# Sixty-four narrow dummy matmuls in place of thirty-two wide ones at the opening of an attention and MLP kernel

## The chip, the cores and the metric

The kernel runs on one core of one Trainium2 chip. The metric is the device time of one execution in microseconds (us); lower is better. Three runs of the kernel before took 103.33, 104.07 and 104.88 us, the median being 104.07. A further execution was taken with the hardware profiler; every row below is from that one.

## The reference

Attention with quadratic sketched features, for 4 batches of 4 heads, 1088 tokens and 32 columns a head, followed by a two-layer network on the 4352 tokens. Cut to what matters:

```python
def phi(x):                                    # S1, S2: 8 x 32
    a = einsum('rd,bhsd->bhsr', S1, x)
    b = einsum('rd,bhsd->bhsr', S2, x)
    return einsum('bhsi,bhsj->bhsij', a, b).reshape(..., 64)
q_p, k_p = phi(q), phi(k)
kv  = einsum('bhsf,bhsd->bhfd', k_p, v)
z   = sum(k_p, axis=2)
num = einsum('bhsf,bhfd->bhsd', q_p, kv)
den = einsum('bhsf,bhf->bhs', q_p, z)[..., None] + 1e-06
x   = (num / den) as 4352 x 128                # heads side by side
h   = x @ w_in                                 # 128 x 2048
out = (h - tanh(h)) @ w_out                    # 2048 x 128
```

Inputs and outputs are float32.

## The kernel before

**How it is staged.** Batch 0 is prepared first, in the opening, in two chunks of queries (16 blocks of 32 tokens, then 18). The network then runs over groups of up to 512 tokens (`layers`), and the attention of batches 1, 2 and 3 is made between the network's matmuls. In the opening, TensorE ("PE") turns the sketches into weights (`sketch`, L605), projects the keys (L704, two parts, "keys0" and "keys1"), spreads S2 (L628), makes the Gram matrix (L729), projects the first queries (L883), folds (L781), and sums key features times values (L748, "sums0" and "sums4"). ScalarE ("ACT") copies that sum (`kvz`, L807), PE transposes the copy (L816), ACT copies it back (`ndw`, L824), and PE multiplies the query features by it (L1007, "nd0" and "nd1", after VectorE's ("DVE") transposes `qpT`, L944). Their result `xT` is cast by ACT and DVE (L1022), and the network's first layer can start: L1114 multiplies by `w_in` into PSUM, ACT takes the tanh (L1124), and L1143 (or L1139 for the last, smaller groups) multiplies by `w_out`. The linear part, h itself times w_out, is folded into one 128 by 128 matrix: `w_in` is transposed in two halves of eight matmuls (L1048), DVE copies each half (L1055), and sixteen matmuls (L1062) make the product, which L1083 applies.

**Dummy matmuls.** `warm` (L597) issues matmuls on a zero tile `wz` whose result nobody reads. `FILLS = 29, 3, 0, 1, 0, 0, 4, 4` says how many stand in each of eight places: 29 before `sketch` ("fill0"), 3 after it ("fill1"), one before the Gram matrix, 4 before the transposes L816 ("fill6") and 4 after them ("fill7"). All are 128 by 128 on 128 columns.

**Who sets the order.** A planner in the kernel's own code (`Program.schedule`, `listed`) builds one list for each engine. For the opening, `LINE` writes each engine's order out by hand, dummies included; from there on the planner chooses by due times and its own cost figures. Its figures also treat TensorE's program as coming in pieces: `PACKET = 256` records a piece, counted from 63 (`count, packets = 63, [0, 0]`), each operation having `ni` records. One matmul of the source is two records, a weight load and a matmul, and for float32 operands four. When the count enters a piece, the planner books the arrival of the piece after the next one, 5,300 ns later in the first 16,500 ns and 3,300 ns later afterwards:

```python
                if count // PACKET != (count + o.ni) // PACKET:
                    packets.append(o.at + (SLOW if o.at < BUSY else FETCH))
                count += o.ni
```

**Queues.** Nearly all loads and stores are issued by SyncE ("SP") in one order. After the loads of batch 0 come w_in (L538) and w_out (L543), then k, q and v of batch 1, which wait for `ndw` of batch 0 (L824). GpSimd ("POOL") casts the second half of w_in (L550) and both halves of w_out (L554); ACT casts the first half of w_in after `ndw`.

Of the kernel before, what the change touches and what calls it, by code (L numbers as in the profile page):

```python
# [51 lines left out]
W_GATE = "wu", 0  # L52
GATE1 = "ndw", 0
WK_POOL = 0
FILLN = 128
FILLS = 29, 3, 0, 1, 0, 0, 4, 4
GPS = ("wk", 1, 0, 0), ("wk", 1, 1, 0), ("qp", 0, 1), ("w_in", 2), ("w_in", 3), ("w_out", 0)
LINE = {
# [343 lines left out]
def bass_polysketch_attn__then__act_tanh_shrink_kernel(nc, q, k, v, S1, S2, moe_w_in, moe_w_out, out):  # L402
    P = Program(nc)

    def sb(name, shape, dtype=F32):
        return nc.alloc_sbuf_tensor(name, shape, dtype).ap()
# [16 lines left out]
    wz = sb("wz", [128, 512], BF16)  # L423
# [47 lines left out]
    ps = nc.alloc_psum_tensor("ps", [128, 8 * 512], F32).ap().rearrange("p (b n) -> p b n", b=8)  # L471
# [125 lines left out]
    def warm():  # L597
        for x, n in enumerate(FILLS):
            for _ in range(n):
                w = 128 if x else FILLN  # L600
                P.op("tensor", 54 * w // 128, lambda e, w=w: e.matmul(  # L601
                    ps[:, 6, 0:w], wz[:, 0:128], wz[:, 0:w], start=True, stop=True), r=[("wz",)], name=f"fill{x}")

    def sketch():
        P.op("tensor", 250, lambda e: e.matmul(  # L605
# [589 lines left out]
    P.bias = BIAS  # L1195
    mark = len(P.ops)
    warm()
    sketch()

# [22 lines left out]
    if LEAD:  # L1222
        for e, names in LINE.items():
            found = [[o for o in P.ops[mark:] if o.eng == e and o.name == n] for n in names]
            line = [o for f in found for o in f]
            assert all(len(f) == (FILLS[int(n[4:])] if n[0][0] == "f" and n[0:4] == "fill" else 1) for n, f in zip(names, found)), names
            for x, y in zip(line, line[1:]):
# [87 lines left out]
```

## Time and profile before

| | |
|---|---|
| three runs, median | 103.33 to 104.88 us, 104.07 us |
| the profiled execution's own time | 104.34 us |
| its span, first to last instruction | 102.2 us (so 2.1 us lie around it) |
| mean granted TensorE clock | 0.983 |
| ACT tanh, L1124 | 138 instructions, 68.9 us busy |
| L1114, 128x512 | 100 matmuls, 35.9 us busy, mean 385 ns |
| L1143, 128x512 | 110 matmuls, 35.4 us busy, mean 379 ns |
| dummy matmuls, L601 | 41 in the trace, 4.7 us busy |
| idle of PE just before L601, "issue" | 1.9 us, once |

"Busy" counts overlapping instructions of an engine once; PE's matmul ends are modelled, so what counts for PE is when one starts after another. "Granted clock" is the share of full speed that the throttle let TensorE run at. An idle time of an engine is put down to what released it; "issue" means that nothing the profile shows released it. Loads of the engines' programs show as DMA queues of the kind "instruction".

### The profile page before, as it was taken

Reading aid. Unit: us, or ns where it says so; the run is one execution under the profiler, and the core shown is the slowest. Engines: PE = TensorE matmul, PEld = TensorE weight load, DVE = VectorE, ACT = ScalarE, POOL = GpSimd, SP = SyncE. Lnnn points to the kernel's source line nnn. Section 1 sums busy time; section 2 is a strip of 40 time slices with the busy share of each in tenths; the row PEclk is TensorE's granted clock in tenths of the full one; section 3 lists DMA queues with packets and bytes.
Section 4 is the critical chain, followed back from the end, with each engine's and each line's share of the span. In section 5 each row is a group of like instructions: output and inputs, shape, how many; then the busy total and the mean of one; then the engine's idle time right before and its main releaser. Section 6 shows DMA issues by size and latency. Waiting matters only on the chain.

```text
span 102.2 us, 3488 instructions
## 1 busy us (share of the span) xinstructions
PE 93.8 (92%) x1505; PEld 56.2 (55%) x1519; DVE 60.7 (59%) x122; ACT 75.1 (74%) x154; POOL 34.5 (34%) x39
## 2 busy tenths in 40 slices
PE   5999389999999999999999999999999999999980
PEld 5888265564365543344447554344343454699980
DVE  3688935499838999973999941591937220042040
ACT  3131613897467892699994969999986999999960
POOL 5646445250195700099989000008800000000000
PEclk9999985999999999999999999999999999999999
DMA  2999899930018799995006150060024006003322
GB/s 49 356 199 291 240 317 375 239 81 10 0 17 244 142 255 201 203 187 76 0 0 227 18 86 3 1 102 0 0 42 65 2 6 96 0 16 61 68 51 77
DMA packets 22911, 11.24 MB, mean 110 GB/s; under 512 B 15728, under 2 KB 21104, under 8 KB 22896
## 3 DMA queue, kind: packets, MB, share of 16 engines
q1 hardware_dynamic: 22464, 10.40, 43.6%
q10 hardware_dynamic: 432, 0.62, 2.0%
q8 instruction: 12, 0.20, 0.8%
q14 instruction: 3, 0.02, 0.1%
HBM read 8.79 MB, written 2.23 MB: 108 GB/s over the span
## 4 chain that ended last, share of the span: by engine, by line
PE 69%; ACT 13%; DVE 10%; issue 4%
PE ps L1114 21%; PE ps L1143 15%; ACT tt L1124 13%; PE ps L1139 5%; PE ps L1007 5%; PE ps L601 4%; PE ps L748 3%; DVE kT L643 2%; DVE qpT L944 2%; PE ps L883 2%; PE ps L1083 2%; PE ps L1048 2%; PE ps L684 2%; PE ps L729 1%; PE ps L704 1%
## 5 line engine op out<-in xcount | busy, mean ns | idle before, releaser
L1124 ACT ACTIVATE tt<-ps 128x512 bf16<-128x512 f32 (+1 forms) x138 | 68.9, 665 | 11.2 <-PE ps L1114 5.2
L1114 PE MATMUL ps<-xT,w_in 128*128 128x512 bf16 x100 | 35.9, 385 | 2.0 <-issue 1.5
L1143 PE MATMUL ps<-tt,w_out 128*128 128x512 bf16 x110 | 35.4, 379 | 0.2 <-issue 0.2
L662 POOL TENSOR_TENSOR wk<-kab 128x1152 f32<-128x1152 f32 (+2 forms) x8 | 15.5, 1933 | 15.4 <-DVE kab L691 13.0
L1114 PEld LDWEIGHTS ps<-xT,w_in 128*128 128x128 bf16 x112 | 9.9, 98 | 15.2 <-ACT tt L1124 7.3
L1143 PEld LDWEIGHTS ps<-tt,w_out 128*128 128x128 bf16 x112 | 10.8, 98 | 11.0 <-issue 0.9
L1166 DVE STREAM_TRANSPOSE osb<-ps 128x512 f32<-128x512 f32 x7 | 5.0, 713 | 12.4 <-PE ps L1143 12.3
L1114 PE MATMUL ps<-xp,w_in 128*128 128x256 bf16 (+1 forms) x64 | 9.5, 246 | 0.1
L983 POOL TENSOR_TENSOR qp<-an,w_out_f 128x1152 f32<-128x1152 f32 x2 | 4.3, 2174 | 13.0 <-DVE an L978 12.9
L1139 PE MATMUL ps<-w_out,tt 128*128 128x128 bf16 x96 | 8.2, 219 | 0.0
L601 PE MATMUL ps<-wz 128*128 128x128 bf16 x41 | 4.7, 285 | 3.1 <-issue 1.9
L989 DVE STREAM_TRANSPOSE qpT<-qp 128x1152 f32<-128x1152 f32 x4 | 5.5, 1368 | 2.5 <-POOL qp L983 2.5
L1007 PE MATMUL ps<-qpT,ndw 32*32 32x288 f32 (+3 forms) x320 | 6.9, 352 | 0.0
L1028 DVE CAST xT<-ps 128x512 bf16<-128x512 f32 x7 | 4.5, 681 | 3.5 <-PE ps L1007 3.5
L1139 PEld LDWEIGHTS ps<-w_out,tt 128*128 128x128 bf16 x96 | 6.4, 98 | 0.1
L933 POOL TENSOR_TENSOR qp<-an,ab 128x512 f32<-128x512 f32 (+2 forms) x3 | 4.5, 1514 | 4.9 <-DVE an L928 4.9
L643 DVE STREAM_TRANSPOSE kT<-kraw 128x256 f32<-128x256 f32 (+3 forms) x10 | 5.6, 602 | 0.7 <-DMA kraw<-in_k_dram 0.7
L1114 PEld LDWEIGHTS ps<-xp,w_in 128*128 128x128 bf16 x64 | 5.0, 98 | 1.5
L851 DVE STREAM_TRANSPOSE qT<-qraw 128x512 f32<-128x512 f32 (+3 forms) x9 | 5.8, 653 | 0.0
L601 PEld LDWEIGHTS ps<-wz 128*128 128x128 bf16 x41 | 3.9, 133 | 3.5 <-issue 2.0
L944 DVE STREAM_TRANSPOSE qpT<-qp 128x512 f32<-128x512 f32 (+2 forms) x6 | 5.6, 954 | 0.1
L1007 PEld LDWEIGHTS ps<-qpT,ndw 32*32 32x32 f32 x320 | 4.0, 103 | 2.7 <-issue 1.2
(101 smaller groups left out, 96.3 us busy)
## 6 DMA issues: line engine op xcount, KB each, us to landing
kraw<-in_k_dram SPq DMA_DIRECT2D x3, 544.0 KB, 4.0
qraw<-in_q_dram SPq DMA_DIRECT2D x3, 544.0 KB, 8.0
w_in_f<-in_moe_w_in_dram SPq DMA_DIRECT2D x4, 256.0 KB, 5.6
w_out_f<-in_moe_w_out_dram SPq DMA_DIRECT2D x2, 512.0 KB, 8.0
out_dram<-osb SPq DMA_DIRECT2D x16, 64.0 KB, 2.5
vx<-in_v_dram SPq DMA_DIRECT2D x6, 144.0 KB, 6.5
vx<-in_v_dram SPq DMA_DIRECT2D x6, 128.0 KB, 7.8
vx<-in_v_dram SPq DMA_DIRECT2D x6, 64.0 KB, 3.0
```

The costliest lines, as they stand in the source:

```text
L601: P.op("tensor", 54 * w // 128, lambda e, w=w: e.matmul(ps[:, 6, 0:w], wz[:, 0:128], wz[:, 0:w], start=True, stop=True), r=[("wz",)], name ...
L643: P.op("vector", dve(hi - lo), lambda e, cb=cb, t0=t0, n=n, lo=lo, hi=hi: e.transpose(out=kT[i][:, t0:t0 + n, cb:cb + 2, :], in_=kraw[i][: ...
L662: return lambda e: e.tensor_tensor(out=wk[:, r, y0:y1, :, :].rearrange("p t h (i j) -> p (t h) i j", i=R), in0=pa[:, :, :, None].to_broadc ...
L851: P.op("vector", dve(hi - lo), lambda e, lo=lo, hi=hi: e.transpose(out=qT[i][:, lo:hi], in_=qraw[i][:, lo:hi]), r=cols("qraw", i, lo, hi), ...
L944: c.t_op = P.op("vector", dve(64 * n), lambda e, r=r: e.transpose(out=qpT[u][:, r, 0:64 * n], in_=qp[u][:, r, 0:64 * n]), r=[("qp", u, r)] ...
L989: c.t_op = P.op("vector", dve(1152), lambda e, r=r: e.transpose(out=qpT[u][:, r, :], in_=qp[u][:, r, :]), r=[("qp", u, r)], w=[("qpT", u, r)])
L1007: ins = e.matmul(ps[32 * h:32 * h + 32, k0 + s, 0:32 * own[s]], ndw[b % 2][32 * s:32 * s + 32, y, 32 * h:32 * h + 32], src, start=(y == 0) ...
L1114: o = P.op("tensor", pe(n), lambda e, jb=jb, bk=bk, y=y: e.matmul(bk[:, n * y:n * y + n], w_in[:, 128 * jb:128 * jb + 128], xs[:, 0:n], st ...
L1124: P.op("scalar", act(m), lambda e, ts=ts, bk=bk, m=m: e.activation(out=tt[:, ts, 0:m], in_=bk[:, 0:m], func=AF.Tanh, scale=-1.0), r=[kb], ...
L1139: P.op("tensor", pe(128), lambda e, jb=jb, ts=ts, o_=o_, at=n * y + at: e.matmul(o_, tt[:, ts, at:at + 128], w_out[:, jb, :], start=False, ...
L1143: P.op("tensor", pe(n), lambda e, jb=jb, ts=ts: e.matmul(acc[:, 0:n], w_out[:, jb, :], tt[:, ts, 0:n], start=(jb == 0 and not g), stop=(jb ...
L1166: P.op("vector", dve(n), lambda e: e.transpose(out=osb[u][:, 0:n], in_=acc[:, 0:n]), r=[ka], w=[("osb", u)], want=due(NJB) + LAG)
```

## The change

The dummies of the first two places become twice as many and smaller: 58 before `sketch` and 6 after it, each with 32 stationary columns (so it writes 32 partitions) and 64 moving columns. The dummies of the other places stay 128 by 128. All 128 rows of the tile still take part.

```diff
-FILLN = 128
-FILLS = 29, 3, 0, 1, 0, 0, 4, 4
+FILLN = 64
+FILLS = 58, 6, 0, 1, 0, 0, 4, 4
...
-                w = 128 if x else FILLN
-                P.op("tensor", 54 * w // 128, lambda e, w=w: e.matmul(
-                    ps[:, 6, 0:w], wz[:, 0:128], wz[:, 0:w], start=True, stop=True), r=[("wz",)], name=f"fill{x}")
+                w = 128 if x > 1 else FILLN
+                m = 128 if w == 128 else 32
+                P.op("tensor", 54 * w // 128, lambda e, w=w, m=m: e.matmul(
+                    ps[0:m, 6, 0:w], wz[:, 0:m], wz[:, 0:w], start=True, stop=True), r=[("wz",)], name=f"fill{x}")
```

The program has 64 records more before the keys, so each later piece of 256 begins 64 records sooner in the work. The planner sees that and lists some instructions elsewhere. In TensorE's list: the second eight transposes of w_in (L1048) go from before the first L1114 to after seven of them (and four L1143); DVE's second copy L1055 follows them, behind the second chunk's `qp` (L938). Before the second chunk's L1007 there are one L1114 and two L1143 more. Of batch 1, the Gram matrix (L729) comes after both L1083 and three L1114 instead of between the two L1083, and DVE's transpose of the first output group (L1166) comes before the Gram matrix's mask (L763) instead of after it. In SP's list the four stores of that output group (L1174) go ahead of the load of k for batch 2 (L517). A few other L1114 and L1143 change places up to the second batch's L1007; from there on, and on POOL throughout, the lists are the same.

## The prediction

> **What bounds the kernel now.** I read the page first, then the chain of waits, then busy time and clock by stretches, then PE's timeline around the longest "issue" wait. From the page:
>
> ```profile
> span 102.2 us, 3488 instructions
> PE 93.8 (92%) x1505; PEld 56.2 (55%) x1519; DVE 60.7 (59%) x122; ACT 75.1 (74%) x154; POOL 34.5 (34%) x39
> ...
> PEclk9999985999999999999999999999999999999999
> ...
> q8 instruction: 12, 0.20, 0.8%
> ...
> PE 69%; ACT 13%; DVE 10%; issue 4%
> ```
>
> PE carries 69% of the chain and is busy for 92% of the span, so a microsecond that it gains before 20 us mostly reaches the end. One slice has half the clock. Twelve program loads went by queue 8, 0.20 MB / 12 = 16 KB each. PE's timeline, with start, duration and the wait in brackets:
>
> ```profile
> 10.24 0.40 PE L601 MATMUL ps<-wz 128*128 128x128 bf16 x4
> 10.80 0.44 PE L816 MATMUL ps<-ident,kvz 128*128 128x128 f32 x2 [0.16 <-ACT kvz L807]
> 11.07 0.28 PE L601 MATMUL ps<-wz 128*128 128x128 bf16 x2
> 13.23 0.27 PE L601 MATMUL ps<-wz 128*128 128x128 bf16 x2 [1.89 <-issue]
> 13.44 1.15 PE L1007 MATMUL ps<-qpT,ndw 32*32 32x128 f32 x64
> ```
>
> Dummies depend on nothing but a zero tile, yet the third of four waited 1.89 us. It is PE's 444th weight load or matmul; with the four waits that stand as records of their own, 447 lie before it, and by the planner's count of 63 ahead and 256 a piece the boundary lies at 449. So I read the wait as PE's program arriving late. The trace's records of queue 8 fit: the first load's packet starts at 10.98 and takes 0.92, and PE goes on 1.33 after its end. The next is at 16.34 for 1.16. Twelve loads agree with some 3,050 PE records / 256 = 11.9 boundaries, one load for each boundary reached, so two pieces were aboard at the start and entering the second asks for the third.
>
> The clock, in stretches cut where the trace's clock records change (columns: stretch and length, busy and count of PE, weight loads, DVE, ACT, POOL, granted clock, DMA share, GB/s):
>
> ```profile
> 4.25:7.67 3.42, 3.33 (x73) 2.55 (x72) 2.90 (x10) 0.80 (x2) 1.52 (x4) 1.00 1.02 226
> 7.67:11.08 3.41, 3.25 (x127) 2.76 (x126) 2.91 (x9) 0.74 (x2) 2.13 (x4) 1.00 0.91 287
> 11.08:14.49 3.41, 1.52 (x70) 1.12 (x67) 1.79 (x4) 1.41 (x3) 1.31 (x3) 1.00 0.94 274
> 14.49:17.91 3.42, 3.20 (x28) 2.28 (x25) 2.16 (x4) 1.41 (x4) 1.84 (x3) 0.50 1.07 354
> ```
>
> The stretch with the wait has PE busy for 1.52 of 3.41, and the clock is halved through exactly the next 3.42; stretches with 3.25 and more keep it. The wait thus costs twice: 1.89 idle, and half of 3.20 = 1.6 of PE's work at half speed.
>
> **The change part by part.** Sums are against the profiled execution, 104.34 (span 102.2 and 2.1 around it), 0.27 above the median of 104.07.
>
> The new dummies. In the trace the old ones start every 107 ns until 4.2 (3.1 in all) and every 55 from 4.7 on: the clock is low up to 4.25. No row has a 32-column matmul alone. Halving the columns gives an estimated 53 ns, 58 x 53 = 3.1, as before. Bounds: 17 ns a pair (L748: 72 in 1.21, on four column groups at a time), so 1.0; and 107, so 6.2. Early gains nothing: keys1 waits for DVE's key transposes, which end at 5.70. Late has 0.2 of slack between keys0 and keys1, then goes on the path, up to +2.9. I take 0, since halving one row is nearer than either end.
>
> The program's pieces. Entering the second piece comes 64 records sooner, at what is now the 63rd pair, in L704 at 6.10, instead of the 95th, L883 at 7.49. PE's sequencer runs ahead: a wait record behind pair 29 ran while pair 13 did, so the request may come some 16 pairs sooner, at pair 47 (5.42); today it cannot come before the wait record at 7.07. From request to resumption it took 13.23 - 7.49 = 5.7 to 13.23 - 7.07 = 6.2. The third piece would thus be there at 11.1 to 12.3; I take 11.7. Further bound: later loads start about 0.3 after their boundary (21.94 to 22.21), which gives 6.1 + 0.3 + 0.9 + 1.3 = 8.6; with DMA 86 to 117% busy here I stay near the loaded row.
>
> The new boundary lies in sums4 (L748), at what is now pair 190, 9.74. The wait becomes 11.7 - 9.7 = 2.0. Today pair 190 to the end of L748 takes 0.57, and from there to the earliest L1007 through kvz, L816 and ndw 1.45 (10.30 to 11.75). So L1007 starts at 13.7 instead of 13.44: **+0.25**. The query side is ready at 12.5 (qpT 11.21 + 1.30) and hides nothing. The loads of batch 1 wait for `ndw`, now 2 us later than 11.64; SP's issue already took 2.30 instead of 0.4 there, so the queue was full, and k lands at 20.97 against its use at 23.42. I count 0; without that cover up to +0.5.
>
> The moved transposes. Eight L1048 fewer stand before the first L1114: at half clock 16 took 1.89, so -0.94; the 0.22 wait ahead of L1114 for the casts of `xT` goes as well, since ACT and DVE finish within the other eight. They return later at full clock, as 16 L1062 do (1.0 for 16): +0.5. Net **-0.66**. The DVE copy that goes with them now follows `qp`, which ends 0.6 sooner with L883 (21.52 - 0.6 = 20.9, by the 18.1 below against 18.72), so it is done at 20.9 + 0.69 = 21.6; by the new list PE needs it near 21.9 (18.1 + 3.8 of rows until L1062): hidden, by 0.3.
>
> The next boundary falls at the end of the second chunk's L883. PE is there at 13.7 + 1.1 + 0.95 + 1.3 (three L1114 at half clock) + 1.0 = 18.1; the fourth piece, asked for at 11.7 and 13.23 to 16.34 + 1.16 + 1.33 = 5.6 on the way, is there at 17.3. At full clock PE would be there near 17.0 and wait 0.3. I book **+0.1**.
>
> The replanned middle. DVE's transpose of the first output (0.71) before the mask lies beside three L1114 (0.65) and L729 (0.3): 0, without them +0.4. Four stores (2.55 of SP issue) ahead of the load of k for batch 2, today issued at 29.54, put its landing near 32.1 + 4.0 = 36.1 against its use at 35.05, with other DVE work able to follow only in order: 0 to +1.0, I take 0 as the first store may start 0.7 sooner and ACT's 2.46 idle at 26.6 shrinks. Sum: +0.25 - 0.66 + 0.1 = -0.3, with the half-clock stretch kept.
>
> One rule speaks against the mechanism itself. The Trainium skill, "Runtime: NRT & Kernel Launch", section "Instruction fetch mechanics", says that the program is refilled in blocks of 256 instructions and that crossing a block is mostly hidden. The 1.89 row disagrees; by the rule the wait had another cause, which is rival four.
>
> **Rivals.** First, the clock does not fall: the wait is cut by the 3.41 grid. On today's grid its idle lies partly before 11.08 (1.3) and partly behind (0.6 and two gaps of 0.3 around L816), so each stretch is about 2.1 busy, between 1.52, which lost the clock, and 3.25, which kept it. That saves 1.6 more: 104.0 - 1.6 = 102.4, or 101.5 if the piece also comes a microsecond sooner, when qpT bounds L1007 at 12.5. Against it, the grid need not lie so in other runs. The Trainium skill, "TensorE: Matmul & The Clock Gate", section "Why this matters for your kernels", allows idle gaps up to about 3 us, by which neither wait would cost the clock and 102.4 would be the rule; the 0.50 row, behind a gap of 1.89, disagrees.
>
> Second, slower: the fourth piece becomes the bound. It is now asked for at 11.7, with w_out (second half lands at 17.50) and then k of batch 1 (20.97) ahead of it in the DMA engines. If its packet starts only at 17.5, it is usable at 17.5 + 1.2 + 1.3 = 20.0, PE waits 1.9 from 18.1, and a second halved stretch costs up to 1.6: 104.0 + 1.9 + 0.8 = 106.7 with half of that stretch. It decides from a packet later than 15.6. For it: a full queue; against: today's packet took 3.1 in the same load.
>
> Third, narrow dummies do not release the clock at 4.25. A quarter of the array's columns works, and no row shows that alone. One stretch more at half clock costs at most 3.33 / 2 = 1.67, less 0.25 of slack: 105.4; two, 3.25 / 2 more: 107.0.
>
> Fourth, the boundary is not where I put it, the wait stays at its dummy: 104.34 - 0.66 = 103.7.
>
> **How the numbers follow.** Forecast 0.50; first rival 0.21; second 0.14; third 0.10; fourth 0.05. The forecast is 104.34 - 0.3 = 104.0, its own range 103.0 to 105.0 by the bounds of the piece's arrival (0.6 either way) and the middle. 2% of 104.07, about what a measurement of this kernel with runs 1.5% apart tells from no change, is 2.1: faster is under 102.0, slower above 106.2. The first rival straddles 102.0 (0.16 below, with a little from the forecast's edge, 0.18); the second mostly lies above 106.2 (0.11), the third half (0.05), stretches that lose the clock twice in the forecast add 0.07: slower 0.23. The rest is 0.59. The range, 102.0 to 106.3, leaves out about a tenth at each end.
>
> **What would show it.** Right: no wait in the four dummies; an "issue" wait inside L748 near 9.8; queue 8's first packet 1 to 2 earlier than 10.98; L1007 at 13.5 to 13.9; L1114 at 15.4 to 16. Wrong: dummies spaced far from 53 ns, a clock that rises only at 7.67, a wait before L1114 behind L883, or a wait gone outright, in which case 104.0 is too high.

## The result and the profile after

The changed kernel took 107.11 us (median of six runs, 106.36 to 107.6) against 103.81 for the kernel before (six runs, 103.33 to 104.88): a ratio of 1.031, 95% interval 1.024 to 1.037. It is slower, and outside the predicted range. In all ratios here executions more than 1.5% above a kernel's fastest are left out, but as most of those had lost clock, which is the subject, medians and means are of all executions. The profiled execution took 106.36 with a span of 104.2, 2.0 longer than before.

Its page, the lines that answer to those shown of before (line numbers from L601 on are one higher than before's):

```profile
span 104.2 us, 3552 instructions
...
PEclk9999976999999999999999999999999999999999
...
q8 instruction: 12, 0.20, 0.8%
...
PE 68%; ACT 10%; DVE 8%; issue 5%; DMA 4%; SPq 2%
```

There are 64 instructions more, and 12 program loads as before. The clock falls once, as before, but DMA and SP's queue are on the chain now. TensorE's timeline (start, duration, wait in brackets):

```profile
1.22 3.08 PE L602 MATMUL ps<-wz 128*32 128x64 bf16 x58 [1.22 <-DVE hmask L567]
...
9.04 0.88 PE L749 MATMUL ps<-wk,vx 128*32 128x64 f32 x48
13.04 0.54 PE L749 MATMUL ps<-wk,vx 128*32 128x64 f32 x24 [3.12 <-issue]
...
15.26 1.81 PE L1008 MATMUL ps<-qpT,ndw 32*32 32x128 f32 x64
17.00 0.88 PE L1049 MATMUL ps<-identb,w_in 128*128 128x128 bf16 x8
17.93 0.59 PE L1115 MATMUL ps<-xT,w_in 128*128 128x512 bf16 x2
```

The dummies take 3.08 / 58 = 53 ns each. The wait left the dummies for L749, where it was put, after 48 of 72 matmuls, and it grew from 1.89 to 3.12. PE goes on at 13.04, 0.19 sooner than before's 13.23, though by the count of records piece two was entered 1.5 sooner (6.01 against 7.49). The first packet of queue 8 starts at 10.77 and takes 0.88 (before 10.98 and 0.92). That the wait is one for the program is borne out by all the profiles: in fifteen of the sixteen with such a wait PE goes on 1.2 to 1.5 after the end of this packet (0.75 in the other). The wait now stands in front of a third of the sums and the chain through kvz and ndw, so L1008 starts 1.82 later than before's L1007 (13.44). The clock by stretches (columns as for before: length, busy and count of PE, weight loads, DVE, ACT, POOL, granted clock, DMA share, GB/s):

```profile
7.34:10.75 3.41, 2.55 (x103) 2.15 (x97) 2.86 (x11) 0.37 (x1) 1.96 (x4) 1.00 0.91 270
10.75:14.17 3.42, 0.97 (x29) 0.71 (x29) 2.15 (x4) 0.37 (x1) 0.95 (x2) 1.00 0.99 294
14.17:17.58 3.41, 3.28 (x76) 2.51 (x77) 0.47 (x2) 1.78 (x4) 2.19 (x3) 0.50 0.85 219
```

The stretch with 0.97 busy is followed by one at half clock; the one with 2.55, in which the wait begins, is not.

Later the trace has one more loss, by ACT's timeline. First the kernel before, then the changed one:

```profile
41.36 1.57 ACT L1124 ACTIVATE tt<-ps 128x512 bf16<-128x512 f32 x3 [2.45 <-PE ps L1114]
```

```profile
43.30 1.08 ACT L1125 ACTIVATE tt<-ps 128x512 bf16<-128x512 f32 x2 [3.19 <-PE ps L1115]
```

This is where the tanh resumes behind batch 1's query product. From there to the end of the span it is 60.8 in the one and 60.9 in the other: what is lost is lost by this point. ACT's waits of 0.3 or more from 21 us to this one come to 0.55 + 2.46 + 0.65 + 0.40 + 2.45 = 6.51 before, and 0.34 + 0.82 + 1.88 + 0.86 + 0.71 + 3.19 = 7.80 after, 1.29 more.

PE's timeline shows where this comes from. These are the projection of the second chunk's queries and that of batch 1's queries, before and changed:

```profile
17.62 1.17 PE L883 MATMUL ps<-wqb,qT 128*64 128x96 f32 x20
29.73 1.26 PE L894 MATMUL ps<-wq,qT 64*64 64x48 f32 x72
```

```profile
18.46 1.05 PE L884 MATMUL ps<-wqb,qT 128*64 128x96 f32 x20
31.60 1.26 PE L895 MATMUL ps<-wq,qT 64*64 64x48 f32 x72
```

From the first to the second it is 12.11 before and 13.14 after. The weight loads between the two show why: in the new list eight transposes L1049 (0.45 at 21.17) and three matmuls of 512 columns more (two L1115 and one L1084, 0.22 each, so 0.65) stand ahead of batch 1's queries. So the 2.0 is made up of 1.82 up to L1008, then -0.98 to the second chunk's L884 (4.18 before, 3.20 after: eight transposes fewer, and 0.8 less of it at half clock), then 13.14 - 12.11 = 1.03 to batch 1's L895, and 72.62 - 72.47 = 0.15 from there to the end.

### The profile page after: what moved, and what is told of

The parts are those of the page before. It is cut to its first block, busy times and chain, and to the rows that moved or that the text cites. A ratio compares the mean times of both kernels' runs of the same rounds, so it can differ in the third digit from the quotient of the medians.

```text
span 104.2 us, 3552 instructions
## 1 busy us (share of the span) xinstructions
PE 93.8 (90%) x1537; PEld 56.4 (54%) x1551; DVE 60.2 (58%) x122; ACT 75.1 (72%) x154; POOL 34.5 (33%) x39
## 4 chain that ended last, share of the span: by engine, by line
PE 68%; ACT 10%; DVE 8%; issue 5%; DMA 4%; SPq 2%
PE ps L1115 21%; PE ps L1144 16%; ACT tt L1125 10%; PE ps L1008 6%; PE ps L1140 5%; DMA kraw<-in_k_dram 4%; PE ps L602 4%; PE ps L749 3%; DVE kT L644 3%; DVE qpT L945 2%; PE ps L884 2%; PE ps L685 2%; PE ps L1084 2%; SPq L1175 2%; PE ps L705 1%
## 5 line engine op out<-in xcount | busy, mean ns | idle before, releaser
L1115 PE MATMUL ps<-xT,w_in 128*128 128x512 bf16 x100 | 35.0, 380 | 2.4 <-issue 1.0
L1144 PE MATMUL ps<-tt,w_out 128*128 128x512 bf16 x110 | 35.1, 379 | 0.2 <-issue 0.2
L1115 PEld LDWEIGHTS ps<-xT,w_in 128*128 128x128 bf16 x112 | 9.9, 97 | 15.2 <-ACT tt L1125 6.7
L1144 PEld LDWEIGHTS ps<-tt,w_out 128*128 128x128 bf16 x112 | 11.0, 98 | 10.9 <-issue 0.4
L1167 DVE STREAM_TRANSPOSE osb<-ps 128x512 f32<-128x512 f32 x7 | 4.9, 707 | 12.4 <-PE ps L1144 12.3
L1115 PE MATMUL ps<-xp,w_in 128*128 128x256 bf16 (+1 forms) x64 | 9.5, 246 | 0.1
L1008 PE MATMUL ps<-qpT,ndw 32*32 32x288 f32 (+3 forms) x320 | 7.6, 380 | 0.3
L749 PE MATMUL ps<-wk,vx 128*32 128x64 f32 x288 | 4.8, 220 | 3.1 <-issue 3.1
L749 PEld LDWEIGHTS ps<-wk,vx 128*32 128x32 f32 x288 | 4.2, 110 | 4.2 <-issue 3.7
L808 ACT COPY kvz<-ps 128x256 f32<-128x256 f32 x4 | 1.4, 374 | 6.8 <-PE ps L749 6.8
L1008 PEld LDWEIGHTS ps<-qpT,ndw 32*32 32x32 f32 x320 | 4.5, 111 | 3.2 <-issue 0.8
L1115 PEld LDWEIGHTS ps<-xp,w_in 128*128 128x128 bf16 x64 | 5.0, 98 | 1.5
```

The source lines that it names most:

```text
L749: ins = e.matmul(ps[32 * h:32 * h + 32, 2, co:co + 64], vx[i][:, h, t, :], wk[:, h // 2, t, h % 2, :], start=(t == 0), stop=(t == 8), tile ...
L1008: ins = e.matmul(ps[32 * h:32 * h + 32, k0 + s, 0:32 * own[s]], ndw[b % 2][32 * s:32 * s + 32, y, 32 * h:32 * h + 32], src, start=(y == 0) ...
L1115: o = P.op("tensor", pe(n), lambda e, jb=jb, bk=bk, y=y: e.matmul(bk[:, n * y:n * y + n], w_in[:, 128 * jb:128 * jb + 128], xs[:, 0:n], st ...
L1144: P.op("tensor", pe(n), lambda e, jb=jb, ts=ts: e.matmul(acc[:, 0:n], w_out[:, jb, :], tt[:, ts, 0:n], start=(jb == 0 and not g), stop=(jb ...
L1167: P.op("vector", dve(n), lambda e: e.transpose(out=osb[u][:, 0:n], in_=acc[:, 0:n]), r=[ka], w=[("osb", u)], want=due(NJB) + LAG)
```

## The experiments

The ratios below compare a kernel's runs with those of the kernel before on the same chip.

A mean granted clock of 1.0, 0.984 or 0.967 counts the stretches of 3.41 us at half clock: none, one or two, since 3.41 x 0.5 / 104 is 1.6%. All executions of these kernels taken together, each row from all its runs:

| kernel | executions | mean us | with 0 / 1 / 2 / 3 stretches | stretches each |
|---|---|---|---|---|
| before | 64 | 104.32 | 39 / 20 / 5 / 0 | 0.47 |
| changed | 18 | 107.06 | 3 / 7 / 8 / 0 | 1.28 |
| records alone | 10 | 106.38 | 0 / 6 / 3 / 1 | 1.5 |
| lists alone | 10 | 105.87 | 5 / 5 / 0 / 0 | 0.5 |

Before's groups have means of 103.47, 105.45 and 106.43, so a stretch costs about (106.43 - 103.47) / 2 = 1.5. The means of ten executions are uncertain by about 0.4 (their scatter of 1.2 over the root of ten). The count has a blind spot: clock records begin with the first rise, so an execution whose clock rose late counts as one that lost nothing. The changed kernel's groups have means of 106.56 (three executions), 106.40 and 107.82, so 0.9 to 3.1 above before's at an equal count: the stretches are a part of its loss, not all of it.

**Records or lists.** The first pair takes the change apart. `records_alone` issues the 64 additional matmuls, but tells the planner of the old number, so every list is as before; `plan_alone` issues the old dummies and tells the planner of the new number, so the lists are the changed kernel's.

```diff
-                w = 128 if x else FILLN
-                P.op("tensor", 54 * w // 128, lambda e, w=w: e.matmul(
-                    ps[:, 6, 0:w], wz[:, 0:128], wz[:, 0:w], start=True, stop=True), r=[("wz",)], name=f"fill{x}")
+                def dummies(e, k=2 if x < 2 else 1, m=32 if x < 2 else 128, w=64 if x < 2 else 128):
+                    for _ in range(k):
+                        ins = e.matmul(ps[0:m, 6, 0:w], wz[:, 0:m], wz[:, 0:w], start=True, stop=True)
+                    return ins
...
+                P.op("tensor", 54, dummies, r=[("wz",)], ni=2 if x < 2 else 2, name=f"fill{x}")
```

This is `records_alone`; in `plan_alone` k, m and w are 1, 128 and 128 throughout, and `ni` is 4 for x < 2.

> The 64 narrow dummies, with every engine's list as in the kernel before (the planner is told of 64 records fewer than there are). Theory A (the third piece of PE's program comes when the DMA engines let it through, near 13.0 us, whatever was asked when; so PE waits longer the sooner it reaches the piece's edge): an issue wait of 3.0 to 3.3 us inside L748, first L1007 near 15.2, 105.2 to 106.0 us. Theory C (the loss is in the replanned middle, where stores go ahead of the load of k): the same wait, but hidden later, 103.8 to 104.4 us. Theory B (on record: the piece comes 5.7 to 6.2 us after its edge is reached) is already against the trace of after, where it came at 13.04.

> The 32 wide dummies of before, with every engine's list as in the changed kernel (the planner is told of 64 records more than there are). Theory A: the wait stays in the dummies with 1.9 us, as before; 103.5 to 104.3 us. Theory C: the load of k for batch 2 lands near 36 and the chain runs through it; 105.5 to 106.5 us with the 1.9 us wait.

Each was run a second time:

> The 64 narrow dummies with the lists of before, once more, as the measure for the next. Theory D (the longer wait costs by itself and through the clock, which it halves for one or two stretches of 3.41 us more often than the wait of before): 1.5 to 2.5 us above the kernel before, a mean granted clock of 0.984 or 0.967 in nearly every execution.

> The wide dummies with the changed kernel's lists, once more, since four runs lay from 103.8 to 107.9. Theory D without a part for the lists: like the kernel before, within 0.7. Theory C (the replanned middle costs in most executions): 1.5 to 3.0 above it.

Measured: records alone 106.17 (105.26 to 107.24, four runs; ratio 1.019, 1.002 to 1.035), then 106.41 (104.97 to 108.13, six; 1.026, 1.014 to 1.039). Lists alone 107.24 (103.83 to 107.87, four, no interval), then 105.25 (104.21 to 107.26, six; 1.019, 1.010 to 1.028). Both cost, in different ways. The records cost the clock: not one of ten executions kept it, 1.0 stretch more than before or some 1.5 us of the 2.1; with one lost stretch they are near the kernel before (105.7 against 105.45, six executions), with two 1.3 above it (three). The lists lose the clock no oftener than the kernel before (0.5 against 0.47), but cost at equal clock: 104.7 against 103.47 with none, 107.0 against 105.45 with one (five executions each).

ACT's waits from 21 us to the resumption behind batch 1's query product, worked out as above, show the lists without the scatter. In eleven profiles with the old lists they come to 6.50 to 6.56, whatever the opening did (`load_last` and `w_in_later` below apart, which have waits of their own); in seven with the new lists to 7.62 to 8.30. From the resumption to the end it is 60.8 to 61.6 in all.

The 1.1 that even the lowest of the seven has more is the work that the new list puts ahead of batch 1's queries. From the second chunk's L883 to batch 1's L894 it is 12.0 to 12.1 in all the profiles with the old lists but one (12.45), and 13.14 in all with the new ones but one that was at half clock in between (13.87); eight transposes and three matmuls of 512 columns, 0.45 + 0.65, are the difference between the lists there. What is gained for it depends on the clock: from the start of the query product to the second chunk's L883 it is 2.73 to 2.75 with the old lists where all of it ran at full clock (five profiles) and 2.50 with the new (`plan_alone`). From that start to the end it is 87.2 to 87.8 in these five and 88.5 in `plan_alone`, which fits the 1.3 between the means without a lost stretch. The lists were not undone at this place alone, so this is read from the traces and not tried.

**Which entry of the lists.** `load_first` is the changed kernel with SP's load of k for batch 2 put ahead of the four stores again; `load_last` is the kernel before with that load behind them.

```diff
         order = self.schedule()
+        line = order["sync"]
+        i = next(i for i, o in enumerate(line) if o.sem == "out0")
...
+        line.insert(i, line.pop(i + 4))
```

This is `load_first`; the last line of `load_last` is `line.insert(i + 3, line.pop(i - 1))`.

> The changed kernel with one thing undone: SP issues the load of k for batch 2 ahead of the four stores of the first output group, as before. All else, records and every other list, as in the changed kernel. Theory A (the loss is the grown wait at the piece's edge): 106.4 to 107.6, no different from the changed kernel. Theory C (in many executions k of batch 2 lands after its use, since the stores go first): 1.0 to 2.0 us below the changed kernel, 105.0 to 106.0.

> The kernel before with one thing changed: SP issues the load of k for batch 2 behind the four stores. The stores are issued at 30.2 to 32.7, so the load starts 3 us later and lands near 37, against a use at 35.05. Theory A: no difference from before beyond 0.5 us. Theory C: 1.0 to 2.5 us slower than before, a wait of DVE for k in the trace.

`after_again`, the changed kernel itself, ran beside them.

> The changed kernel once more, beside the next two on one chip, as their measure: 106.4 to 107.6 us as in its first six runs, and 2.5 to 3.5 above the kernel before.

Measured: `load_first` 106.96 (105.88 to 107.41, six runs; 1.030, 1.023 to 1.036), the changed kernel beside it 107.83 (106.13 to 109.11, six; 1.0245, 1.015 to 1.034): 0.9 apart, within the scatter. `load_last` 105.92 (103.75 to 108.99, six, no interval). In the trace the load's place shows plainly. `load_last`, timelines of DVE and PE:

```profile
35.55 0.78 DVE L647 STREAM_TRANSPOSE kT<-kraw 128x576 f32<-128x576 f32 x1 [1.53 <-DMA kraw<-in_k_dram]
```

```profile
38.90 1.55 PE L1011 MATMUL ps<-qpT,ndw 32*32 32x288 f32 x64 [1.40 <-DVE qpT L948]
```

DVE's transpose of k waits 1.53 for the load, the transposes of `qpT` behind it are as late, and PE's query product waits 1.40. ACT's waits come to 8.02, 1.51 more than before: in the old lists all of the late load reaches the end. In the new lists ACT's sum is 7.62 with the load first (`load_first`) and 7.68 to 8.30 with it last: the load's place is 0.1 to 0.7 of it, and 1.1 stands without it.

The new lists also show a wait that no old list shows: in the changed kernel's trace L1115 waits 0.88 for the casts of `xT` at 42.87, because one L1144 stands between the query product and it, where before three stood (PE's weight loads show them all; the timeline's matmuls lack one record at each place). `after_mended` puts two back; `after_third`, the changed kernel, ran beside it.

```diff
         order = self.schedule()
+        line = order["tensor"]
+        i = [i for i, o in enumerate(line) if o.name == "nd0" and o.ni == 128][1]
+        line[i - 2:i + 1] = line[i], line[i - 2], line[i - 1]
```

> The changed kernel with one place of TensorE's list put back: two w_out matmuls stand behind batch 1's query product again, as in the kernel before, so that three stand between it and the first layer's matmuls, not one. Theory: the lists cost time at this place, where the changed kernel's TensorE waits 0.88 for the casts of xT (42.87 in its profile; the kernel before has 0.16 there). By it the wait falls to 0.2 or less and the mean of many executions is 0.9 below the changed kernel beside it. Rival: that wait is made good later, because ACT's tanh or the casts set the pace behind it; then the wait goes and the mean stays within 0.3.

> The changed kernel again, to be compared with the run beside it on the same chip: 107.3 on average over its twelve executions so far, with 1.5 stretches of half clock in each.

Measured: `after_mended` 106.97 (105.16 to 109.23, eight runs; 1.021, 1.014 to 1.029), `after_third` 106.36 (105.67 to 107.72, six; 1.026, 1.020 to 1.032); the means are 107.1 and 106.5, with 1.4 and 0.8 lost stretches. No gain, as the rival had it, though its 0.3 is finer than these means can tell. First PE's timeline of `after_third`, then of `after_mended`:

```profile
40.52 1.55 PE L1008 MATMUL ps<-qpT,ndw 32*32 32x288 f32 x64 [0.63 <-DVE qpT L945]
42.94 0.82 PE L1115 MATMUL ps<-xT,w_in 128*128 128x512 bf16 x3 [0.55 <-DVE xT L1029]
```

```profile
42.39 1.55 PE L1011 MATMUL ps<-qpT,ndw 32*32 32x288 f32 x64 [1.06 <-DVE qpT L948]
```

The two matmuls taken from ahead of the query product leave a wait there, 1.06, in place of 0.63 and 0.55 at two places. ACT's sum is 8.30 and 8.29. DVE sets the pace here: in both, its transpose of k waits 0.59 for the load before it can go on to `qpT`.

**When the third piece comes.** Three more kernels. Two, with before's lists, change how many records stand before the keys: `records_192` issues four matmuls of 32 by 32 for each dummy, 192 records more than before; `fewer` issues eight dummies of 464 columns and one of 384, 46 fewer. `w_in_later` is `records_alone` with the loads of w_in moved behind a later event; its lists are before's in the opening, but behind it eight transposes of w_in have moved here too.

```diff
-FILLS = 29, 3, 0, 1, 0, 0, 4, 4
+FILLS = 8, 1, 0, 1, 0, 0, 4, 4
...
-WI_GATE = ("kab", 0, 0), ("kab", 0, 0)
+WI_GATE = ("wu", 0), ("wu", 0)
```

The first pair of lines is of `fewer`, the second of `w_in_later`.

> 128 dummies of 32 by 32 columns in the first two places, 192 records more than before, the lists as before. The second piece's edge moves from L883 to before the keys (asked for by 4.4 us), the third's to near 9.3 in L748. Theory A: the program load's packet still starts near 10.8, PE goes on near 13.0, the wait is 3.5 to 3.8 us. Theory B: the packet starts 1.5 us or more sooner than 10.8 and the wait is 2.2 us or less.

> Nine wide dummies (eight of 464 columns, one of 384) in the first two places, the same columns in all and 46 records fewer, the lists as before. The third piece's edge moves behind the four dummies into the first L1007, which qpT allows from 12.0 to 12.5. Theory A: the piece comes near 13.0 all the same, the wait shrinks to 0.5 to 0.9 us, 102.3 to 103.3 us. Theory B: the second piece's edge is reached 0.8 later, the third piece comes near 14.0, the wait is 1.5 us or more and the time no better than before.

> The 64 narrow dummies with the lists of before in the opening, and the four loads of w_in issued with w_out at 8.4 us instead of 6.2. Theory A in its form on the load (the program's packet, asked for near 6, queues with the transfers then in the DMA engines, w_in among them): the packet starts at 9.0 or sooner instead of 9.7 to 10.8, PE goes on by 11.3. If the packet is paced by something else (a clock of its own, or PE's own progress): still 9.7 to 10.8.

Measured: 104.99 (103.06 to 106.32, four runs), 105.08 (102.89 to 107.19, four) and 110.2 (109.95 and 110.45), against 104.47 (102.93 to 105.42, seven) beside the first two and 104.15 (102.78 to 108.29, twelve) beside the third. With 192 more records the packet starts at 4.86 and there is no wait at the edge, but k is late (DVE, then PE):

```profile
6.50 0.77 DVE L646 STREAM_TRANSPOSE kT<-kraw 128x256 f32<-128x256 f32 x2 [1.21 <-DMA kraw<-in_k_dram]
```

```profile
7.32 0.80 PE L707 MATMUL ps<-wkm,kT 128*64 128x64 f32 x20 [1.25 <-DVE kT L646]
```

The second half of k landed at 6.47 here, and at 4.3 to 4.4 in eighteen other profiles. That the program load pushed it back is not shown: in `narrow_look2` below it landed at 6.27, with no program load before 11.62.

With fewer records the packet starts at 11.42 and the wait is 0.63 within L1007, on from 13.76. In `w_in_later` (PE's timeline)

```profile
11.29 0.54 PE L751 MATMUL ps<-wk,vx 128*32 128x64 f32 x24 [0.53 <-issue]
...
20.95 0.48 PE L886 MATMUL ps<-wqb,qT 128*64 128x96 f32 x2 [4.20 <-issue]
```

the packet starts at 8.93, ahead of the first load of w_in (issued at 9.27), and the wait at this edge is 0.53; `records_alone`, which in the opening differs by w_in's place alone, has 9.68 (for a transfer of 1.46), 12.50 and 2.65. This fits a program load that is delayed by the data in the DMA engines, but it is one profile each, and in `covered_wide` below the packet starts at 7.78 with w_in in its old place. With w_in moved behind, the fourth piece is late: its packet starts at 18.5, 7.2 after PE went on at this edge (1.5 to 4.3 in the other profiles with a wait), and PE waits 4.20 within the second chunk's L886. Over the nineteen profiles other than that of `records_192` the packet started anywhere from 7.8 to 12.4, and in the sixteen in which PE waited for it, it went on at 11.3 to 14.8. The request's place explains none of that spread: with the old number of records PE went on at 12.05 to 14.45 (seven profiles, mean 13.2), 4.3 to 6.3 after piece two was entered; with 64 more, and w_in in its place, at 12.49 to 14.80 (seven, mean 13.3), 6.5 to 8.0 after. Only in `records_192`, which entered piece two at 3.75, was the packet early.

`after_again` shows the late end, its packet at 12.37 (PE's timeline, then the stretches):

```profile
14.80 0.87 PE L749 MATMUL ps<-wk,vx 128*32 128x64 f32 x24 [4.15 <-issue]
```

```profile
10.11:13.52 3.41, 0.55 (x40) 0.42 (x29) 3.24 (x8) 0.00 (x0) 1.19 (x2) 1.00 0.95 279
13.52:16.94 3.42, 2.14 (x33) 1.69 (x33) 0.15 (x1) 0.43 (x2) 1.23 (x2) 0.50 0.82 226
16.94:20.35 3.41, 3.10 (x76) 2.33 (x75) 0.92 (x3) 1.72 (x4) 2.08 (x2) 0.50 0.60 177
```

A wait of 4.15 that reaches into the next stretch leaves that one at 2.14 busy, at half speed, and a second one is lost. This fits the 0.8 of a stretch that the changed kernel loses more than before: the wait has grown, and with it the chance that two stretches fall short. Two further profiles with 64 more records, `records_again` and `after_mended`, lost two in the same way.

**Keeping the clock through the wait.** `records_covered` and `covered_wide` put eight dummies of 512 columns just ahead of the new edge, at the end of `sums0`, so that TensorE is busy longer before it stops; they keep before's lists and the changed kernel's record count, with narrow dummies of 64 columns and five old ones in the first, 36 narrow ones of 16 columns and twenty old ones in the second.

```diff
+                    for _ in range(8 if b == 0 and t0 == 0 else 0):
+                        ins = e.matmul(ps[:, 6, 0:512], wz[:, 0:128], wz[:, 0:512], start=True, stop=True)
```

> As the one before, but eight of the 64 dummies stand between the two halves of L748, just ahead of the piece's edge, and have 512 columns, so that PE has about 1.7 us of work while it waits for its program. Records ahead of the edge, and all lists, are the same; the program still comes when it comes, near 13.0. Theory D: the clock stays (0.984 to 1.0 in most executions), 0.8 to 1.8 us below the kernel with the bare wait. Theory A alone (only the wait's own length counts): no difference beyond 0.4.

> 64 dummies and the lists of before, with eight of 512 columns ahead of the edge inside L748 as in records_covered, but of the other 56 the last 20 before the sketch are wide (128 by 128) and 36 tiny (32 by 16). So the clock rises as before and stays through the wait; what is left of the change is the longer wait itself, its edge in L748 instead of in the dummies. Theory D: 1.0 to 2.0 above the kernel before with its covered wait (103.4), so 104.4 to 105.4, and below records_covered (106.1) if theory E holds. If only the clock matters: 103.2 to 104.0.

`covered_before` covers the kernel before: the eight dummies around L816 all go behind it, six of them with 512 columns, as many records as before.

```diff
-FILLS = 29, 3, 0, 1, 0, 0, 4, 4
+FILLS = 29, 3, 0, 1, 0, 0, 0, 8
...
-                w = 128 if x else FILLN
+                w = 512 if x == 7 and i < 6 else 128
```

> The kernel before, with six of its dummies of 512 columns between L816 and the edge (and none ahead of L816), as many records. Theory D: its wait no longer halves the clock in some executions, 0.2 to 0.8 below the kernel before. Theory A alone: no better, or 0.2 worse.

Measured: `records_covered` 106.23 (104.51 to 107.42, six runs; 1.021, 1.007 to 1.034) and `covered_wide` 106.7 (103.19 to 107.36, six, no interval), with a mean granted clock of 0.996 to 1.0 in all twelve executions. But against `records_again` the first gains 0.2 in the median (0.4 in the mean) and the second nothing in the median (0.4 in the mean, on another chip), and in the profiled executions something else went wrong (`records_covered`, PE's timeline and the stretch over it):

```profile
5.46 2.19 PE L713 MATMUL ps<-wkm,kT 128*64 128x64 f32 x36
```

```profile
6.45:9.86 3.41, 3.41 (x71) 2.77 (x67) 1.67 (x5) 0.80 (x2) 2.49 (x3) 1.00 0.71 181
```

The keys' 36 matmuls took 2.19 instead of the 1.48 of other profiles: TensorE still ran at half speed. The trace's first clock record comes only at 13.27 (15.15 in `covered_wide`), and before it the granted-clock column reads 1.00. So these two don't part the cost of the wait from that of the clock.

`covered_before` took **103.43 (102.43 to 104.44, twelve runs)** and lost no stretch in any of the twelve; beside it the kernel before took 104.62 (102.43 to 107.55, seventeen runs) and lost one or more in nine. The ratio is 1.002 (0.997 to 1.0075), and before's eight executions without a lost stretch have a mean of 103.4, as `covered_before` has over all twelve: at equal clock the kernels are the same, and the 1.2 between the medians is the stretches that are no longer lost. PE's timeline and its stretches:

```profile
14.45 0.27 PE L601 MATMUL ps<-wz 128*128 128x128 bf16 x2 [1.26 <-issue]
```

```profile
10.08:13.49 3.41, 2.57 (x72) 1.59 (x62) 3.24 (x8) 1.92 (x4) 1.21 (x2) 1.00 0.96 296
13.49:16.90 3.41, 2.39 (x83) 2.02 (x84) 1.14 (x4) 0.40 (x2) 1.22 (x2) 1.00 1.04 295
```

The wait is still there, 1.26, but no stretch is below 2.39 busy, and none is halved. This is the best version found.

**Narrow or wide.** `narrow_alone` gives the old number of dummies the narrow form: 32 stationary columns on 128 moving ones.

```diff
-                    ps[:, 6, 0:w], wz[:, 0:128], wz[:, 0:w], start=True, stop=True), r=[("wz",)], name=f"fill{x}")
+                m = 32 if x < 2 else 128
...
+                    ps[0:m, 6, 0:128], wz[:, 0:m], wz[:, 0:128], start=True, stop=True), r=[("wz",)], ni=2, name=f"fill{x}")
```

> The kernel before with the dummies of the first two places narrowed to 32 stationary columns and nothing else: as many of them, 128 moving columns each, as many records, all lists as before. Theory E (narrow dummies release the clock later in some executions, as in the one of records_covered that stayed at half speed up to 13.27): 0.5 to 2.0 above the kernel before in the mean, the first rise of the clock behind 7.0 us in some executions. If narrowness costs nothing: within 0.5 of the kernel before.

> One more profile of the narrow dummies alone: when does the clock rise? Theory E: behind 7.0 us in some of the three profiles. Otherwise between 3.9 and 7.0, as with the wide ones.

> A third profile of the narrow dummies alone, for the same question: theory E has the first rise behind 7.0 us in some of the three, the other case always between 3.9 and 7.0.

Measured: 103.76 (102.84 to 107.11, twelve runs; ratio 1.004, 1.0005 to 1.008) beside 103.27 (102.53 to 106.24, seventeen); two further single executions, each profiled, took 102.62 and 104.74. The means are 104.2 and 103.9, so the form costs little if anything: 0.3, uncertain by 0.5. In the three profiles the clock first rises at 5.73, 5.15 and 13.31. Over all kernels the late rise (13.3 and more) came in three profiles, all with dummies of 32 columns among them, and in none of the six with wide ones alone: too few to call it shown. In the one of `narrow_look2` PE also waited 0.61 within the keys, for the half of k that landed at 6.27.

## Why the prediction was wrong, point by point

**The new dummies at 0: right.** 53 ns each, and the clock rises at 3.93 (before 4.25). Rival three did not come true in this profile.

**The edge in L748 near 9.74: right.** The rows show it after 48 of 72 at 9.9, the fourth rival fell, and queue 8's load answers to it.

**"The third piece would thus be there at 11.1 to 12.3; I take 11.7": wrong.** It was there at 13.04, and at 12.49 to 14.80 in four later profiles with the same records and the same lists but for one place. The step took one time from request to resumption, 5.7 to 6.2, from one profile, and moved it with the request. What the runs show in its place is a time that is not fixed, 4.3 to 8.0, and a packet whose start is spread over more than 4 us: PE went on at 13.2 in the mean with the old number of records and at 13.3 with 64 more. Asking 1.5 sooner bought 0.2 in this execution, so the wait was 3.12, not 2.0, and L1007 moved by +1.82, not +0.25. Of these 1.57, 1.34 is the piece; the rest is the chain behind it, which took 2.22 to L1008 instead of 2.02, with its end at half clock. This is the step that failed first and most.

**"With the half-clock stretch kept": wrong, for the mean.** In the two profiled executions one stretch is lost in each, as predicted. But over many executions the kernel before loses 0.47 of one and the changed kernel 1.28. The prediction carried the 1.6 of its profiled execution through as if every execution had it, and gave 0.07 to losing it twice. At 1.5 a stretch this is 0.8 x 1.5 = 1.2 of the 2.7 between the means, the lists' 1.3 being most of the rest. The first rival, that the clock would not fall, ran the wrong way in the mean: the wait grew. Its condition, some 2.1 busy in each stretch, would mostly have kept the clock: over all profiles 1.64 was enough, but 2.12 lost it once.

**The replanned middle at 0, bounds 0 to +1.0 and +0.4: wrong, though in the profiled execution within the bounds.** From the second chunk's L883 to batch 1's queries 1.03 was added (1.14 against the old lists at full clock), 0.45 of it the returned transposes, which were booked elsewhere, and 0.65 the three matmuls more that now stand ahead; so the middle itself is +0.6, not 0. The prediction had seen matmuls go ahead there, but took them as cover for DVE's transpose; batch 1's chain begins behind them, and from L894 on all takes its time as before (72.47 and 72.62). With the late loads of k ACT's waits grew by 1.1 to 1.8. Over whole executions the lists alone cost 104.7 - 103.47 = 1.3 where no stretch is lost, the moved transposes' gain included, which at full clock is only 0.23 from the query product to the second chunk's L883. The reason given, that "the first store may start 0.7 sooner", held as far as it goes: the stores were issued at 30.59 against 30.16, 0.43 later, with a query product 1.82 later. But the load of k behind them went out at 32.60 instead of 29.54, and four of the seven profiles with new lists show waits of 0.34 to 0.59 for it.

**The moved transposes at -0.66: near.** From the start of the query product to the second chunk's L883 it took 4.18 before and 3.20 after, -0.98, where -1.16 was reckoned for the transposes; about 0.4 of that is less time at half clock. Their return took 0.45, where 0.5 was reckoned: -0.53 in all. The wait of 0.22 for the casts of `xT` was none: three weight loads of L1114 stand there for two matmuls in the timeline, so one matmul's record is missing.

**Batch 1's loads at 0 and the fourth piece at +0.1: right here.** DVE's transpose of k at 24.46 has no wait, and nothing waits behind L884; the second packet starts at 16.17. The second rival's mechanism shows all the same in `w_in_later`, with a wait of 4.20 behind a packet at 18.5.

The predicted sum was -0.3. With the measured terms of the profiled execution it is +1.82 (L1007) - 0.98 (to the second chunk's L883) + 1.03 (to batch 1's L894) + 0.15 (behind it) = +2.0, against 104.2 - 102.2 = 2.0. The base was also a lucky one: before's profiled execution, 104.34, lies 1.1 below the mean of the twenty that lost one stretch.

**On the two rules.** The Trainium skill, "Runtime: NRT & Kernel Launch", section "Instruction fetch mechanics", has block crossings mostly hidden; the runs show waits up to 4.2 at one crossing, and that the wait moves when records are added, so the rule does not hold in this opening. The Trainium skill, "TensorE: Matmul & The Clock Gate", section "Why this matters for your kernels", allows gaps up to about 3 us; a gap of 1.89, in a stretch with 1.52 busy, lost the clock here.

What stays open: what sets the packet's start, how many executions hide a late first rise of the clock, and what the longer wait costs apart from the clock.

## What to carry to other kernels

A wait for an engine's program is not shortened by the amount by which it is asked for sooner: here, with the DMA engines 91 to 99% busy, asking some 1.4 sooner left the mean resumption at 13.3 against 13.2. Such a wait is better placed where little depends on the work behind it, with long filler ahead of it so that the clock survives (`covered_before`). Work moved out of a busy opening is not free where it lands: it stands ahead of whatever chain starts behind it. A change of one number in a planner's input is two changes, the instructions and every list made from them, and each is worth a run alone. Count the clock's lost stretches over many executions before a profiled one is taken for the kernel.

## What the runs showed of the hardware that was not expected

Stretches of 3.41 us, cut at each trace's clock records, in all twenty profiles: where a stretch at full clock had TensorE busy for 1.53 us or less (fifteen stretches), the next ran at half clock; where it was busy for 1.64 or more, the next ran at full clock too, but for one of 2.12 (`records_192`). At half clock 2.13, 2.48 and 2.74 were followed by another half stretch, 3.07 and more (eleven stretches) by full clock. In `records_again` (stretches)

```profile
13.57:16.98 3.41, 2.74 (x50) 2.03 (x58) 0.04 (x1) 1.07 (x3) 1.30 (x3) 0.50 0.85 245
16.98:20.40 3.42, 3.36 (x80) 2.83 (x65) 1.49 (x4) 1.08 (x3) 2.00 (x2) 0.50 0.81 253
```

2.74 busy at half clock was followed by another half stretch, 3.36 by full clock (from 20.40). The first rise is another matter: in `records_covered` the stretch with 3.41 busy, at half speed by the length of its matmuls, did not bring it.
